# Widening an accumulating DMA to all tap pairs in a dynamic convolution followed by a tanh-shrink feed-forward layer

## Chip, cores, metric

One core of one Trainium2 chip. The metric is the device time of one execution in microseconds. The kernel before takes 768.71 us (median of 3 runs, 767.7 to 769.29).

## The reference, cut to what matters

```python
w = softmax(weight_gen, axis=-1)             # (8, 4096, 8 heads, 7 taps)
x_unf = windows of 7 past positions of x     # x: (8, 4096, 192), zeros ahead of each sequence
x = einsum('bshk,bskhg->bshg', w, x_unf).reshape(32768, 192)
h = x @ w_in                                 # (192, 2048)
out = (h - tanh(h)) @ w_out                  # (2048, 192)
```

## The kernel before

Tokens come in 32 superblocks of 1024 (8 per partition). For each, ScalarE takes the exponential of the tap weights, VectorE finishes the softmax, and GpSimd multiplies x by the weights, one product tile per tap. Seven product tiles must be summed and transposed. TensorE does both with matmuls against the identity that accumulate in PSUM ("transposes" below, line label `pc`). From superblock 4 on, an accumulating DMA first adds most of the odd taps' products into the even ones', so that TensorE has fewer to sum.

```python
ACC = NPAIR * J * D - J * R                      # all pairs but one third of the last one
...
            if k == K - 2 and in_pairs:          # in products(n), on GpSimd, after the last odd tap
                nc.gpsimd.dma_start(
                    out=even[:].rearrange("p i c j h g -> p (i c j h g)")[:, 0:ACC],
                    in_=odd[:].rearrange("p i c j h g -> p (i c j h g)")[:, 0:ACC],
                    accum_op=mybir.AluOpType.add, max_dma_last_dim=4096)
...
            groups = [even[:, i] for i in range(NPAIR)] + [last[:]]
            prods_of[n] = [groups + ([odd[:, NPAIR - 1]] if c == NC - 1 else []) for c in range(NC)]
```

Each f tile of the first matmul (16 a superblock) goes to one of three PSUM buffers, is read by tanh (ScalarE) and a subtraction (VectorE), which frees the buffer. The transposed sums use the same three buffers: chunk 2 (the "last third") between matmuls of the second layer, then chunks 0 and 1 (the "two thirds") in a burst. The softmax also parks its reciprocals in the first of these buffers.

```python
    for n in range(NTOT):
        if n + 3 < NTOT:
            load_x(n + 3)
        for p in range(J):
            gemm1(n, 2 * p); gemm1(n, 2 * p + 1)           # f tiles 2p, 2p+1
            ...
            if n + 3 < NTOT:
                if p == 1: softmax_exp(n + 3)
                if p == 1 and n + 4 < NTOT: load_wg(n + 4)
                if 2 <= p <= 5: softmax_sum(n + 3, (p - 2) * 2, (p - 1) * 2)
                if p == 6: softmax_recip(n + 3, 0, J // 2)
            if p < 6 or n == NTOT - 1: gemm2((n - 1) * J + p)
            if p == 0 and 1 < n < NTOT - 2: products(n + 2, behind=last_sub[0])
            ...
        gemm2((n - 1) * J + 6, between=between)            # last-third transposes of n + 1 in between
        conv(n + 1, (0, 1))                                # two-thirds transposes: 64 in a burst
        gemm2((n - 1) * J + 7, 0, FILL)
        if n + 3 < NTOT:
            softmax_recip(n + 3, J // 2, J)
            softmax_norm(n + 3, pcs[0][:, 0])              # copy to PSUM, then scale
        gemm1(n, NFT - 2); ...; gemm1(n, NFT - 1); ...
```

The softmax here doesn't subtract the row's maximum and nothing guards it: scores larger than these inputs give would overflow.

## Time and profile before

| | before |
|---|---|
| time, median | 768.71 us |
| span of the profiled execution | 765.5 us |
| steady superblock (start of its first tanh to the next one's) | 22.775 us |
| superblocks 1 / 2 / 3, the ramp | 28.30 / 23.91 / 22.97 us |
| accumulating DMA, issue to landing | 8.8 us |

Superblock times are read from the trace as the start of a superblock's first tanh to the start of the next one's. In the steady part nearly all agree within 0.01 us, so a change of 0.1 us per superblock is plain in the trace.

### The profile page before, as it was taken

The numbers are of one execution on the slowest core, as the hardware profiler recorded it, in microseconds if no ns is written. First come the engines' busy times: TensorE is split into PE (matmuls) and PEld (weight loads), VectorE is DVE, ScalarE is ACT, GpSimd is POOL, SyncE is SP. The second block draws the span as 40 slices with busy tenths as digits, with TensorE's granted clock in tenths as the row PEclk, the third lists the DMA queues.
The fourth block names the chain that finished last, engine by engine and source line by source line (L and its number), as shares of the span: only waits on it lengthen the run. The fifth ranks groups of instructions, "written<-read, shape, count | busy, mean of one in ns | idle before, by whom it ended". The sixth has DMA issues, their size and how long they took to land.

```text
span 765.5 us, 32560 instructions
## 1 busy us (share of the span) xinstructions
PE 739.1 (97%) x14848; PEld 564.6 (74%) x14848; DVE 681.1 (89%) x765; ACT 642.0 (84%) x869; POOL 668.9 (87%) x262
## 2 busy tenths in 40 slices
PE   4798999999999999999999999999999999999997
PEld 2476777777777777777777777777777777777777
DVE  7986899999999999999999999998999999998893
ACT  4886788888888888888888888888888888888882
POOL 8999999999999999999999999999999999999000
PEclk9999999999999999999999999999999999999999
DMA  8911467665555775545775555766555676542312
GB/s 217 236 42 57 134 171 183 182 175 121 124 151 163 182 181 117 130 150 156 182 184 129 131 144 147 182 179 151 133 131 149 173 182 169 118 122 64 81 43 85
DMA packets 25399, 110.04 MB, mean 144 GB/s; under 512 B 4671, under 2 KB 9519, under 8 KB 21294
## 3 DMA queue, kind: packets, MB, share of 16 engines
q1 hardware_dynamic: 14718, 77.03, 29.1%
q0 software_dynamic: 10544, 30.94, 25.5%
q8 instruction: 116, 1.90, 1.0%
q14 instruction: 21, 0.17, 0.1%
HBM read 54.52 MB, written 25.17 MB: 104 GB/s over the span
## 4 chain that ended last, share of the span: by engine, by line
PE 79%; DVE 15%; ACT 3%; issue 1%; DMA 1%; DVEq 0%
PE ph L308 39%; PE obank L342 37%; DVE gt L320 9%; ACT th L319 3%; DVE wsm L193 2%; PE pc L267 2%; DVE zr L163 2%; PE po L377 1%; DMA x_t<-in_x_dram 1%; DVE pc L169 1%; DVE odd L219 0%; DMA wg_t<-in_weight_gen_dram 0%; DVE even L219 0%; DVE zsum L154 0%; DVE obank L193 0%
## 5 line engine op out<-in xcount | busy, mean ns | idle before, releaser
L320 DVE TENSOR_TENSOR gt<-ph,th 128x1024 bf16<-128x1024 f32 x512 | 604.9, 1220 | 62.0 <-ACT th L319 52.8
L319 ACT ACTIVATE th<-ph 128x1024 f32<-128x1024 f32 x512 | 500.3, 1021 | 66.7 <-PE ph L308 64.8
L342 PE MATMUL obank<-w_out,gt 64*128 64x192 bf16 x7936 | 399.9, 243 | 0.8 <-ACT out_sb L361 0.4
L308 PE MATMUL ph<-convT,w_in 64*128 64x512 bf16 x3072 | 384.4, 378 | 7.9 <-DVE gt L320 2.9
L342 PEld LDWEIGHTS <-gt 64*128 64x128 bf16 x7936 | 343.6, 94 | 65.5 <-issue 0.9
L219 POOL TENSOR_TENSOR even<-x_t,wsm 128x1536 bf16<-128x1536 f32 x93 | 272.6, 2931 | 27.5 <-DVE gt L320 27.2
L219 POOL TENSOR_TENSOR odd<-x_t,wsm 128x1536 bf16<-128x1536 f32 x93 | 272.6, 2931 | 0.0
L308 PEld LDWEIGHTS <-w_in 64*128 64x128 bf16 x3072 | 163.6, 94 | 115.6 <-issue 11.7
L219 POOL TENSOR_TENSOR last<-x_t,wsm 128x1536 bf16<-128x1536 f32 x32 | 105.9, 3308 | 0.0
L361 ACT ACTIVATE out_sb<-obank 128x192 f32<-128x192 f32 x248 | 81.6, 329 | 7.0 <-PE obank L342 2.6
L291 ACT ACTIVATE convT<-pc 128x512 bf16<-128x512 f32 (+1 forms) x63 | 50.7, 807 | 30.1 <-PE pc L267 30.1
L267 PE MATMUL pc<-ident,even 64*128 64x64 bf16 x2256 | 56.1, 191 | 0.6 <-issue 0.4
L267 PEld LDWEIGHTS <-even 64*128 64x128 bf16 x2304 | 53.2, 96 | 1.4 <-issue 0.7
L234 POOL DMA_DIRECT2D even<-odd x28 | 33.7, 1205 | 8.7 <-POOL odd L219 8.7
L267 PE MATMUL pc<-ident,last 64*128 64x64 bf16 x752 | 26.8, 192 | 9.4 <-POOL last L219 9.2
L154 DVE TENSOR_REDUCE zsum<-e_t 128x16 f32<-128x112 f32 (+1 forms) x116 | 31.5, 271 | 3.0 <-ACT e_t L143 3.0
L267 PEld LDWEIGHTS <-last 64*128 64x128 bf16 x768 | 19.7, 96 | 9.7 <-POOL last L219 9.2
L143 ACT ACTIVATE e_t<-wg_t 128x448 f32<-128x448 f32 x32 | 18.5, 578 | 6.5 <-DMA wg_t<-in_weight_gen_dram 6.5
L267 PE MATMUL pc<-ident,odd 64*128 64x64 bf16 x464 | 18.5, 198 | 3.7 <-issue 2.6
L193 DVE TENSOR_TENSOR wsm<-e_t,pc 128x448 f32<-128x448 f32 x28 | 17.4, 622 | 3.1 <-DVE pc L169 0.2
L267 PEld LDWEIGHTS <-odd 64*128 64x128 bf16 x512 | 15.1, 100 | 4.6 <-issue 2.7
L163 DVE RECIPROCAL zr<-zsum 128x32 f32<-128x32 f32 (+1 forms) x58 | 16.6, 327 | 0.1
(27 smaller groups left out, 64.5 us busy)
## 6 DMA issues: line engine op xcount, KB each, us to landing
x_t<-in_x_dram SPq DMA_DIRECT2D x31, 1344.0 KB, 9.0
even<-odd POOLq DMA_DIRECT2D x28, 1024.0 KB, 8.8
out_dram<-out_sb SPq DMA_DIRECT2D x31, 768.0 KB, 11.6
wg_t<-in_weight_gen_dram SPq DMA_DIRECT2D x32, 224.0 KB, 7.8
x_t<-in_x_dram SPq DMA_DIRECT2D x1, 768.0 KB
w_out<-in_moe_w_out_dram POOLq DMA_DIRECT2D x1, 768.0 KB, 8.8
out_dram<-out_sb SPq DMA_DIRECT2D x4, 192.0 KB, 1.8
x_t<-in_x_dram SPq DMA_DIRECT2D x1, 504.0 KB
```

What stands on the lines that cost most here:

```text
L154: nc.vector.reduce_sum(out=zsum_of[n][:, j0 * H : j1 * H], in_=e_of[n][:, j0:j1].rearrange("p j h k -> p (j h) k"), axis=AX.X,)
L163: nc.vector.reciprocal(zr_of[n][:, j0 * H : j1 * H], zsum_of[n][:, j0 * H : j1 * H])
L193: return eng.tensor_mul(wsm.rearrange("p j h k -> p (j h) k"), e_t[:].rearrange("p j h k -> p (j h) k"), zr.rearrange("p (n o) -> p n o", ...
L219: mul = eng.tensor_mul(dst[k][:, :, j0:j1].rearrange("p c j h g -> p j h c g"), x_t[:, k + j0 : k + j1, :].rearrange("p j (h c g) -> p j h ...
L234: nc.gpsimd.dma_start(out=even[:].rearrange("p i c j h g -> p (i c j h g)")[:, 0:ACC], in_=odd[:].rearrange("p i c j h g -> p (i c j h g)" ...
L267: nc.tensor.matmul(pc[r][:, col : col + R] if home else pc[:, r, col : col + R], lhsT=prods[c][gi][r * R : (r + 1) * R, c, 2 * j : 2 * j + ...
L291: nc.scalar.activation(out=out, in_=pc[:, :, 0:cols].rearrange("p r (cj t) -> p r cj t", t=R), func=ACT.Copy,)
L308: nc.tensor.matmul(ph[:, r, :], lhsT=w_in[r * R : (r + 1) * R, c, f * P : (f + 1) * P], rhs=convT[r * R : (r + 1) * R, c, :], start=(c == ...
L319: last_act[0] = nc.scalar.activation(out=th[:], in_=ph_f, func=ACT.Tanh)
L320: last_sub[0] = nc.vector.tensor_sub(gt[:], ph_f, th[:])
L342: mm = nc.tensor.matmul(po[:, 0:D], lhsT=g_of[n][f][r * R : (r + 1) * R, col : col + P], rhs=w_out[r * R : (r + 1) * R, f, :], start=(r == ...
L361: last_act[0] = nc.scalar.activation(out=out_sb[:, j, :], in_=po[:, 0:D], func=ACT.Copy)
```

## The change

Intent: the DMA adds all three odd tiles into the even ones, as three pieces of 1536 elements a partition instead of two of 2048, so that the last third needs 32 transposes and not 40. With it come two changes of order: the softmax pieces, and the load of the tap weights (cut from the diff below), move one or more p earlier, and the x loads made in superblocks 1 to 3 go to the end of the superblock, behind the convolution.

```diff
-    ACC = NPAIR * J * D - J * R
...
-                    out=even[:].rearrange("p i c j h g -> p (i c j h g)")[:, 0:ACC],
-                    in_=odd[:].rearrange("p i c j h g -> p (i c j h g)")[:, 0:ACC],
+                    out=even[:].rearrange("p i c j h g -> p i (c j h g)"),
+                    in_=odd[:].rearrange("p i c j h g -> p i (c j h g)"),
...
-            prods_of[n] = [
-                groups + ([odd[:, NPAIR - 1]] if c == NC - 1 else []) for c in range(NC)
-            ]
+            prods_of[n] = [[even[:, i] for i in range(NPAIR)] + [last[:]]] * NC
...
+    LATE = (1, 2, 3)
...
-        if n + 3 < NTOT:
+        if n + 3 < NTOT and n not in LATE:
             load_x(n + 3)
...
-                if p == 1:
+                if p == 0:
                     softmax_exp(n + 3)
...
-                if 2 <= p <= 5:
-                    softmax_sum(n + 3, (p - 2) * 2, (p - 1) * 2)
-                if p == 6:
-                    softmax_recip(n + 3, 0, J // 2)
+                if 1 <= p <= 3:
+                    softmax_sum(n + 3, (p - 1) * 3, min(p * 3, J))
+                if 4 <= p <= 5:
+                    softmax_recip(n + 3, (p - 4) * JH, (p - 3) * JH)
...
-            softmax_recip(n + 3, J // 2, J)
...
+        if n in LATE:
+            load_x(n + 3, last_conv[0])
```

More of the change, by code (lines that the diff above doesn't have):

```diff
@@ L81 @@
     last_exp = {}
+    last_conv = {}
     first_halo = {}
@@ L242, in products @@
         if in_pairs:
-            groups = [even[:, i] for i in range(NPAIR)] + [last[:]]
-            prods_of[n] = [
-                groups + ([odd[:, NPAIR - 1]] if c == NC - 1 else []) for c in range(NC)
-            ]
+            prods_of[n] = [[even[:, i] for i in range(NPAIR)] + [last[:]]] * NC
         else:
@@ L290, in conv_out @@
             else:
-                nc.scalar.activation(
+                last_conv[0] = nc.scalar.activation(
                     out=out,
@@ L498 @@
             if n + 3 < NTOT:
-                if p == 1:
+                if p == 0:
                     softmax_exp(n + 3)
-                if p == 1 and n + 4 < NTOT:
+                if p == 0 and n + 4 < NTOT:
                     load_wg(n + 4)
-                if 2 <= p <= 5:
-                    softmax_sum(n + 3, (p - 2) * 2, (p - 1) * 2)
-                if p == 6:
-                    softmax_recip(n + 3, 0, J // 2)
+                if 1 <= p <= 3:
+                    softmax_sum(n + 3, (p - 1) * 3, min(p * 3, J))
+                if 4 <= p <= 5:
+                    softmax_recip(n + 3, (p - 4) * JH, (p - 3) * JH)
             if p < 6 or n == NTOT - 1:
```

## The prediction

> **What bounds the kernel now.** I read the page first, then the chain of waits inside one steady superblock, then the ScalarE timeline of that superblock against one near the end, then the ramp.
>
> ```profile
> PE 739.1 (97%) x14848; PEld 564.6 (74%) x14848; DVE 681.1 (89%) x765; ACT 642.0 (84%) x869; POOL 668.9 (87%) x262
> ...
> PE 79%; DVE 15%; ACT 3%; issue 1%; DMA 1%; DVEq 0%
> ```
>
> TensorE is busy nearly always, but a fifth of the chain that ends last is not TensorE. So not every matmul removed is time removed. The next view is the chain of waits between 309.9 and 321 us (columns: start, us, what), the end of superblock 12; superblocks repeat every 22.775 us there (the first tanh of each to the next).
>
> ```profile
> 311.23 0.67 PE ph L308 x6
> ...
> 311.91 1.03 ACT th L319
> ...
> 312.97 2.35 DVE gt L320 x2
> 315.33 0.48 DVE zr L163 x2
> ...
> 315.90 0.24 DVE pc L169
> ...
> 316.23 0.63 DVE wsm L193
> ...
> 316.91 0.82 PE ph L308 x6
> ```
>
> The transposes (L267) run in this stretch and are **not on the chain**: it leaves TensorE after f tile 12 of the first matmul, goes through tanh, two subtractions, two reciprocals, the copy and the softmax scaling, and returns with f tile 15. That tile needs the PSUM buffer in which the softmax keeps its reciprocals, and TensorE waits 0.36 us for it (24 such waits, 8.5 us in the waits view). Next the ScalarE timeline of superblock 12 (start, us, ...):
>
> ```profile
> 311.91 1.94 ACT L319 ACTIVATE th<-ph 128x1024 f32<-128x1024 f32 x2 [0.32 <-PE ph L308]
> ...
> 315.40 1.02 ACT L291 ACTIVATE convT<-pc 128x1024 bf16<-128x1024 f32 x1 [0.36 <-PE pc L267]
> 316.32 1.02 ACT L319 ACTIVATE th<-ph 128x1024 f32<-128x1024 f32 x1
> 317.77 1.02 ACT L319 ACTIVATE th<-ph 128x1024 f32<-128x1024 f32 x1 [0.44 <-PE ph L308]
> ...
> 321.61 1.02 ACT L319 ACTIVATE th<-ph 128x1024 f32<-128x1024 f32 x1 [0.32 <-PE ph L308]
> ```
>
> and of superblock 30, which has no softmax to do for a later one:
>
> ```profile
> 721.88 1.94 ACT L319 ACTIVATE th<-ph 128x1024 f32<-128x1024 f32 x2 [0.32 <-PE ph L308]
> ...
> 725.36 1.02 ACT L291 ACTIVATE convT<-pc 128x1024 bf16<-128x1024 f32 x1 [0.36 <-PE pc L267]
> 726.28 2.17 ACT L319 ACTIVATE th<-ph 128x1024 f32<-128x1024 f32 x2
> ...
> 731.44 1.02 ACT L319 ACTIVATE th<-ph 128x1024 f32<-128x1024 f32 x1 [0.32 <-PE ph L308]
> ```
>
> From tanh of tile 12 to tanh of the next superblock's tile 2 is 9.70 us with the softmax and 9.56 without. The trace thus already holds a superblock without the 0.36 us wait, and it is only **0.14 us** shorter. Last, the chain in superblock 1, and under it the busy times of 61.6 to 65 us (clock is the 0.54):
>
> ```profile
> 57.83 1.21 PE pc L267 x83
> 59.04 2.61 issue
> 61.65 0.95 PE pc L267 x29
> ...
> 61.60:65.00 3.40, 3.35 (x55) 2.58 (x56) 0.00 (x0) 1.78 (x2) 3.40 (x2) 0.54 0.27 72
> ```
>
> Superblock 1 takes 28.30 us. TensorE stops 2.61 us among transposes whose operands were ready (GpSimd had finished them at 54.2) and then runs at half clock.
>
> **What the Trainium skill says.** (1) "Runtime: NRT & Kernel Launch", Instruction fetch mechanics: instructions arrive in 16 KiB blocks over the sequencer's own DMA queue, mostly hidden. The page agrees on the size (116 instruction packets, 1.90 MB); at 59.04 it is, as I read it, not hidden. (2) "DMA: Bandwidth & Descriptors", Issuing engines are not separate DMA queues: all transfers share the same 16 engines. The x load is issued at 54.27, lands at 59.83, and from 55.5 to 59 the DMA share is 0.83; an instruction packet runs only at 59.37. (3) "TensorE: Matmul & The Clock Gate", Part 1: an idle window of about 3.4 us halves the clock. The trace has one such halving between ramp and end, 3.41 us long, right after this pause. (4) The DMA page again, SDMA does more than copy: the adder takes at most 2048 elements a piece. The build agrees: the accumulate is 128x2x2048 before, 128x3x1536 after.
>
> **The change part by part.**
>
> Transposes. 64 of them run from 314.26 to 315.19, so 14.5 ns each (two row tiles at once; the 191 ns of the groups view is latency). Eight fewer is 0.116 us of TensorE in the last-third sums, 28 x 0.116 = 3.2 us if it all counted. It lands just before the two-thirds sums, which need the PSUM buffer of tile 12. VectorE frees that at 314.20 and TensorE starts at 314.26: it is already tied. Start earlier and it waits. Worth about 0.01 us a superblock.
>
> Reciprocals. In the new order the three sums (3, 3 and 2 rows) and two reciprocals go to the pairs p=1 to 5. After tile 13's subtraction (ends 315.33) only copy and scaling are left. They end at about 316.20 instead of 316.85, so tile 15 starts when TensorE gets there: tile 14 at 315.38 + 0.645 + 7 pairs x 0.0826 = 316.60, not 316.91; 0.31 us gained. Two tiles later it meets the next wait: the next superblock's tile 1 needs tile 14's buffer, whose chain (transposes done, 1.02 ScalarE copy, 1.02 tanh, 1.22 subtraction, ending 318.60) is untouched. TensorE could be there at 318.48 but starts at 318.65, against 318.79 before. So 0.14 us stays: the same number that superblock 30 shows.
>
> Do the moved VectorE pieces fit? A pair period is 2.615 us. The sum of two rows took 0.26 and left 0.084 idle. Three rows are 168 elements; between 0.26 for 112 and 0.61 for 448 that is 0.32, so about 0.02 is left. A reciprocal of 0.26 to 0.34 just fits. The exponential (0.58) at p=0 falls in a ScalarE hole of the new order. No charge.
>
> Steady sum: 28 x 0.14 = 3.9 us.
>
> Accumulate. 1.18 MB for 1.05 and 24 pieces an engine for 16. Landing was 8.8 us; scaled by bytes and piece counts I estimate 9.5 to 10. It is issued at 317.22 and needed near 335.5: hidden. Its 1.2 us on GpSimd hardly depends on the pieces (the w_out load with 2048 rows took 1.23), and GpSimd idles 1.13 us a superblock waiting for its pace.
>
> Late x loads (superblocks 1, 2, 3). The loads go behind the convolution, so the DMA engines are free while superblock 1's transposes drink instructions fastest. Without trouble that superblock should take 22.775 + 64 extra transposes x 14.5 ns = 23.7 us: 4.6 us are in play, 2.61 of pause, 1.7 of half clock (half of 3.41), the rest small. GpSimd reaches these tiles at 75.3, 96.5 and 118.0; the loads should land near 70, 88 and 114 by adding 9 us to the new issue points, so nothing waits. I count three quarters: 3.5 us.
>
> Sum: 768.7 - 3.9 - 3.5 = **761.3 us**.
>
> **Rivals.** *All transposes count*: 3.2 us from the transposes and 8.5 from the wait, plus the ramp, 753 us. Against it: superblock 30 shows the wait removed and 0.14 gained. *The pause is not fetch contention*: then only the steady part comes, 765 us. For it: the profile says only "issue". Against it: later transposes at the same rate do not pause (no issue wait over 0.3 us from 100 to 650 us). *GpSimd or the accumulate becomes the bound*: GpSimd's work repeats every 21.6 us in the ramp; if descriptor generation doubled to 2.4, it would be 22.8 and eat the gain, 766 to 769. A small form is likely: with superblock 1 shorter, superblock 3 wants the first accumulate at about 103, and it landed at 101.56 already before growing; a wait under 1 us, once. *VectorE slips* because a 3-row sum overruns its hole: up to 0.05 us a pair, recovered at p=0: 1 us.
>
> **Range and chances.** Steady part 3 to 5, ramp 0 to 4.6, less up to 1.5 for the last two rivals: 758 to 766 in 8 of 10. A 2% gain needs below 753.6, all of the first rival: 0.03. Slower than 2% needs a new stall each superblock: 0.01.
>
> **What would show it.** Right: steady period 22.63 us; the wait of tile 15 on the scaling gone; new short waits of TensorE on subtractions at tile 1 and ahead of the two-thirds sums; no 2.6 us issue pause and no half clock near 60 us. Wrong: a period near 22.3 (transposes count), a pause that survives or moves, transposes waiting for the accumulate, or GpSimd without its 1.1 us pace idle.

## The result

The changed kernel takes 765.28 us (median of 4 runs, 764.66 to 766.12) against 768.27 us for the kernel before on the same chip; ratio 0.996, 95% interval 0.9943 to 0.9978. The gain is 3.0 us where 7.4 were forecast.

The page of the changed kernel, the lines that answer to the first two of the prediction:

```profile
PE 739.3 (97%) x14624; PEld 572.9 (75%) x14624; DVE 676.4 (89%) x737; ACT 642.2 (84%) x869; POOL 671.0 (88%) x262
...
PE 82%; POOL 13%; DMA 2%; issue 2%; ACT 0%; SPq 0%; DVE 0%; POOLq 0%
```

There are 224 matmuls fewer, VectorE has left the chain, and GpSimd (POOL) has come onto it. TensorE's busy time has not fallen at all. The ScalarE timeline of a steady superblock (start, us, what, and in brackets the idle time before and who ended it):

```profile
290.23 1.94 ACT L316 ACTIVATE th<-ph 128x1024 f32<-128x1024 f32 x2 [0.32 <-PE ph L305]
...
293.71 1.02 ACT L288 ACTIVATE convT<-pc 128x1024 bf16<-128x1024 f32 x1 [0.47 <-PE pc L264]
294.63 2.18 ACT L316 ACTIVATE th<-ph 128x1024 f32<-128x1024 f32 x2
...
299.79 1.94 ACT L316 ACTIVATE th<-ph 128x1024 f32<-128x1024 f32 x2 [0.16 <-PE ph L305]
```

Tanh of tile 12 to tanh of the next superblock's tile 2 is 299.79 - 290.23 = 9.56 us, the forecast value, and the period is 22.63 us from superblock 8 on. So the steady half of the forecast came exactly. The rest is in the ramp. Superblock times in us, from the two traces:

```
superblock            1      2      3      4      5      6      7   8 and on
before            28.30  23.91  22.97  22.77  22.77  22.78  22.77  22.775 (two at 22.92)
changed           25.29  24.09  22.67  24.02  22.67  26.36  22.46  22.63
difference        -3.02  +0.19  -0.31  +1.25  -0.11  +3.58  -0.31  about -0.14 each
```

Superblocks 7 to 28 gain 3.58 us together; 29 and 30 lose 0.16. The start and superblocks 1 to 6, taken together, **lose** 1.8 us, against a forecast gain of 3.5: what superblock 1 gave, superblocks 4 and 6 took back. (The two profiled executions differ by 1.6 us and not by 3.0; the kernel before's was the quickest of its first four, 767.27 us. Only the profiled ones can be taken apart.) The chain of waits of the changed kernel at the end of superblock 6 (start, us, what), and the busy times of the 3.4 us after it (0.50 is the granted clock, 0.02 the DMA share):

```profile
175.91 0.47 PE pc L264 x25
176.39 1.92 issue
178.30 0.74 PE pc L264 x39
...
179.00:182.40 3.40, 3.40 (x34) 2.08 (x28) 0.76 (x1) 2.05 (x2) 3.40 (x2) 0.50 0.02 5
```

This is the picture that superblock 1 of the kernel before showed: TensorE stops amid its burst of transposes for nothing the profile knows of, then runs 3.41 us at half clock. It has moved, not gone. Superblock 4 has two smaller losses. First the waits of GpSimd from 92 to 112 us, then the chain from 126 to 136 us:

```profile
POOL odd L219 <- DMA even<-odd: 3.8, 1, 3.8
```

```profile
118.56 9.66 DMA even<-odd
128.21 0.14 issue
...
129.82 0.38 PE pc L264 x26
130.20 0.77 issue
130.96 0.73 PE pc L264 x38
```

GpSimd, about to write the odd products of superblock 5 at 100.1 us, waits 3.8 us until the accumulating DMA of superblock 4 lands, a wait that the kernel before has not. So it issues the next DMA at 118.6 us and not 114.4, and that one lands at 128.2, after TensorE has come for its sums. The DMA also lands later than before, counted over all of them (issue lines of the changed kernel: KB each, median us from issue to landing; 8.8 us before):

```profile
even<-odd POOLq DMA_DIRECT2D x28, 1152.0 KB, 10.4
```

### The profile page after: what moved, and what is told of

Its sections match the earlier page's. It is cut to its first block, busy times and chain, and to the rows that moved or that the text cites. A ratio compares the mean times of both kernels' runs of the same rounds, so it can differ in the third digit from the quotient of the medians.

```text
span 763.9 us, 32085 instructions
## 1 busy us (share of the span) xinstructions
PE 739.3 (97%) x14624; PEld 572.9 (75%) x14624; DVE 676.4 (89%) x737; ACT 642.2 (84%) x869; POOL 671.0 (88%) x262
## 4 chain that ended last, share of the span: by engine, by line
PE 82%; POOL 13%; DMA 2%; issue 2%; ACT 0%; SPq 0%; DVE 0%; POOLq 0%
PE obank L340 38%; PE ph L305 38%; PE pc L264 5%; POOL odd L219 5%; POOL even L219 5%; POOL last L219 2%; PE po L375 1%; DMA even<-odd 1%; DMA x_t<-in_x_dram 1%; POOL wsm L193 0%; POOL w_in L415 0%; POOL w_out L402 0%; SPq L96 0%; DVE out_sb L387 0%; ACT ot L386 0%
## 5 line engine op out<-in xcount | busy, mean ns | idle before, releaser
L305 PE MATMUL ph<-convT,w_in 64*128 64x512 bf16 x3072 | 392.5, 379 | 4.7 <-DVE gt L317 2.5
L340 PEld LDWEIGHTS <-gt 64*128 64x128 bf16 x7936 | 351.5, 94 | 59.0 <-ACT th L316 0.9
L305 PEld LDWEIGHTS <-w_in 64*128 64x128 bf16 x3072 | 172.9, 94 | 107.7 <-issue 19.6
L264 PE MATMUL pc<-ident,even 64*128 64x64 bf16 x2256 | 59.4, 191 | 3.7 <-issue 3.0
L264 PEld LDWEIGHTS <-even 64*128 64x128 bf16 x2304 | 56.6, 96 | 7.8 <-issue 4.2
L234 POOL DMA_DIRECT2D even<-odd x28 | 36.1, 1289 | 8.6 <-POOL odd L219 8.6
L154 DVE TENSOR_REDUCE zsum<-e_t 128x24 f32<-128x168 f32 (+2 forms) x88 | 27.5, 312 | 2.8 <-ACT e_t L143 2.8
L163 DVE RECIPROCAL zr<-zsum 128x32 f32<-128x32 f32 (+1 forms) x58 | 20.3, 350 | 0.1
L375 PE MATMUL po<-w_out,gt 64*128 64x192 bf16 x256 | 11.0, 243 | 0.0
L375 PEld LDWEIGHTS <-gt 64*128 64x128 bf16 x256 | 10.8, 93 | 0.0
## 6 DMA issues: line engine op xcount, KB each, us to landing
even<-odd POOLq DMA_DIRECT2D x28, 1152.0 KB, 10.4
```

The costliest lines, as they stand in the source:

```text
L154: nc.vector.reduce_sum(out=zsum_of[n][:, j0 * H : j1 * H], in_=e_of[n][:, j0:j1].rearrange("p j h k -> p (j h) k"), axis=AX.X,)
L163: nc.vector.reciprocal(zr_of[n][:, j0 * H : j1 * H], zsum_of[n][:, j0 * H : j1 * H])
L234: nc.gpsimd.dma_start(out=even[:].rearrange("p i c j h g -> p i (c j h g)"), in_=odd[:].rearrange("p i c j h g -> p i (c j h g)"), accum_o ...
L264: nc.tensor.matmul(pc[r][:, col : col + R] if home else pc[:, r, col : col + R], lhsT=prods[c][gi][r * R : (r + 1) * R, c, 2 * j : 2 * j + ...
L305: nc.tensor.matmul(ph[:, r, :], lhsT=w_in[r * R : (r + 1) * R, c, f * P : (f + 1) * P], rhs=convT[r * R : (r + 1) * R, c, :], start=(c == ...
L340: mm = nc.tensor.matmul(po[:, 0:D], lhsT=g_of[n][f][r * R : (r + 1) * R, col : col + P], rhs=w_out[r * R : (r + 1) * R, f, :], start=(r == ...
```

## The experiments

**Theory A**, formed on these lines: the missing gain went into the one 3.8 us wait of GpSimd, which put the later DMAs into the transposes of superblocks 4 and 6. Why the wait is new: the kernel before also read `odd` with TensorE, much later than the DMA does; now the DMA alone reads it. In the built program the odd products of superblock 5 wait for that DMA, where before they waited for TensorE. As I read it, the two-buffer pool hands superblock 5 the buffer whose reading ended first in program order, now that of superblock 4. **Rivals**: B, the wider DMA starves TensorE's instruction fetch by itself; C, the transposes do count; D, the pauses have nothing to do with loads.

**1. Two odd buffers by parity** (changed kernel otherwise).

```diff
-        odd = ppool.tile([P, NPAIR, NC, J, H, GC], BF16, name="odd")
+        odd = ppool.tile([P, NPAIR, NC, J, H, GC], BF16, name="odd", tag=f"odd{n % 2}", bufs=1)
```

> The changed kernel, with the odd products in two buffers chosen by the superblock's parity, so that superblock 5 takes the buffer of superblock 3 and not that of superblock 4, which the accumulating DMA is still reading. Theory A (the missing gain went into one 3.8 us wait of GpSimd for that DMA, which put the later DMAs into the transposes of superblocks 4 and 6): the 3.8 us wait is gone, superblocks 4 and 6 take 22.6 to 22.9 us each and not 24.0 and 26.4, and the time falls from 765.3 to about 760.3. Rival B (the 12% more bytes and the smaller pieces of the DMA delay the instruction fetch by themselves): the wait goes but pauses remain, 764 to 766.

Measured: 763.69 us, ratio to before 0.9927 (0.9906 to 0.9947). GpSimd's wait is gone (no such line from 64 to 111 us) and superblock 6 takes 22.47 us. But superblock 4 takes 24.55 and superblock 5 24.02, with pauses of TensorE of 1.96 and 1.55 us from one matmul's start to the next. The buffer is the cause of the wait; theory A as a whole is too simple, since the pauses only moved and the expected 760.3 us did not come.

**2. The softmax order alone** (kernel before, with the p conditions of the diff above).

> The kernel before, with only the softmax pieces moved (exponential at p=0, sums at p=1 to 3, reciprocals at p=4 and 5); all 24 last-third transposes per tap stay. Theory A: the whole steady gain is from this, superblock period 22.63 to 22.64 us and not 22.775, about 764.4 us (3.9 less than before). Rival C (the transposes carry part of the gain): period between 22.65 and 22.775.

Measured: 765.62 us, ratio 0.9952 (0.9933 to 0.9971). Steady period 22.64 us with all its transposes: 0.14 us less than before, and 0.004 more than the changed kernel. The steady gain is all from the softmax order. Superblock 1 fell by 2.05 us and superblock 2 rose by 3.51, with a new pause and half clock at 87.3 us, although no load was moved.

**3. The wide accumulate alone** (kernel before, with the DMA and `prods_of` lines of the diff).

> The kernel before, with only the accumulate widened to all the pairs and its 8 transposes dropped. Theory A: the steady period stays 22.775 us, GpSimd waits once for the DMA of superblock 4 before it writes the odd products of superblock 5, and the time is not below before: 767.5 to 773. Rival C: the 8 transposes of 14.5 ns count, period 22.66, 765.

Measured: 770.96 us, ratio 1.002 (1.000 to 1.004). Steady period 22.775 us, as before: **eight transposes fewer are worth nothing**. GpSimd's wait is there, from its waits between 84 and 112 us:

```profile
POOL odd L219 <- DMA even<-odd: 4.0, 1, 4.0
```

Superblocks 4 and 5 take 24.16 and 24.31 us. The part that names the change gains nothing by itself; what it costs, 1.0 us between the medians with an interval that touches no change, is in the ramp.

**4. The late x loads alone** (kernel before, with LATE).

> The kernel before, with only the x loads of superblocks 1 to 3 put behind the convolution. Theory A: the 2.6 us pause and the half clock of superblock 1 go, that superblock takes about 25.3 us and not 28.3, steady period 22.775, 765.3 us. Rival D (the pause has nothing to do with the load): superblock 1 keeps 28 us, 768.3.

Measured: 765.21 us, ratio 0.9947 (0.9924 to 0.9969). Superblock 1 takes 24.73 us; its chain of waits:

```profile
59.30 1.21 PE pc L268 x83
60.51 0.49 issue
61.00 0.59 PE pc L268 x29
```

The pause at the same transpose is 0.49 us and not 2.61, so rival D falls: the load made most of it (superblock 1 also began 1.5 us later here; theory E below has the same border in ten traces). Superblocks 2, 4 and 5 give back 0.5 us each, with small pauses.

**Theory A2**, after these: TensorE's pauses come when its bursts meet DMA traffic whose times GpSimd sets; an earlier TensorE meets it elsewhere.

**5. Softmax order and late loads, narrow accumulate** (2 and 4 together).

> The changed kernel without its widened accumulate (softmax pieces moved and x loads of superblocks 1 to 3 put late; the 8 transposes stay). Theory A2 (the gain of the early superblocks is given back where TensorE's transposes meet DMA traffic whose times GpSimd sets; the wide accumulate adds to that traffic): superblocks 4 and 5 take about 23.2 us each as with the late loads alone, steady 22.64, about 762.5 us, so faster than the changed kernel although it has 224 more transposes. Rival (the 12% wider accumulate does not matter, TensorE is simply early): 24 us or more in superblocks 4 and 5, 764 us or more.

Measured: 762.92 us, ratio 0.9936 (0.9906 to 0.9965); one of its four runs took 766.81 us and the others 762.83 to 763.00, so a single execution can stand 4 us apart. Superblocks 4 and 5 take 23.12 and 23.19 us, as expected. The changed kernel's ratio of 0.996 came from another call, so I don't rank the two by it; superblocks 4 to 6 sum to 68.9 us here and 73.1 us there.

**6. Late loads in superblocks 4 and 5 too, on 1, and 7. on 5** (`LATE = (1, 2, 3, 4, 5)`).

> The changed kernel with the parity buffers and with the x loads of superblocks 4 and 5 late as well. Theory A2: without an x load in flight the pauses of superblocks 4 and 5 (1.96 and 1.55 us with the parity buffers alone) shrink below 0.5 us, both superblocks take 22.6 to 23.1 us, total about 761. Rival (the accumulate or the store alone starves the fetch): the pauses stay, 763.5.

> The narrow accumulate with the softmax pieces moved and the x loads of superblocks 1 to 5 late. Theory A2: no pause over 0.5 us after superblock 2, superblocks 4 and 5 at 22.6 to 22.9 us, about 760.5 us, the fastest of all here; the steady period is 22.64 as with the wide accumulate. Rival: pauses elsewhere, 762 or more.

Measured: 766.99 us, ratio 0.9978 (0.9958 to 0.9997), and 765.39 us, ratio 0.9954 (0.993 to 0.9979). In both, superblocks 4 and 5 take 22.63 or 22.64 us, no pause left: that step holds. But GpSimd now starts superblock 8 late, 6.9 us in the wide one and 5.0 us in the narrow one. In the wide one x itself landed at 160.6 us, before GpSimd was free at 161.9; the small DMA of zeros that follows it at the start of a sequence landed at 168.7, and there the wait ended. GpSimd's next DMAs move (186.3 us for the fifth in the wide one, 180.5 in experiment 1), and pauses come in superblocks 6 to 9 (23.48, 26.41, 23.50, 24.51 us in the wide one). The total I expected was wrong by 5 to 6 us.

**8. x loads put into the bursts on purpose** (experiment 1, and for n of 8 and on `load_x(n + 3, last_act[0])` at p = 4).

> The changed kernel with parity buffers and with the x loads of superblocks 8 on put on purpose at p=4, so that each is in flight while the transposes run. Theory A2: pauses by issue of 0.5 to 2.5 us appear in the transposes of most superblocks that showed none, the period rises from 22.63 to between 23 and 26 us, the time to 775 to 840 us. Rival D (the pauses are not made by loads): period stays 22.63, 764 us.

Measured in one look, so its state is unknown: 765.39 us. The median period stays 22.63 us, with two pauses over 0.5 us after the ramp (1.04 us at 269 us and 0.55 us at 566 us), though the load is issued at 308.9 in a superblock whose burst is near 313. So a load in flight is not enough, and theory A2 falls in this form: something else must coincide.

**Theory E.** The trace also records the packets by which instructions come. Over all 17 traces I took every gap of over 0.5 us between the starts of two matmuls, from 55 to 740 us, that the profile puts down to issue. There are 48. A few, with the end of the last instruction packet before it:

```
kernel            TensorE resumes   last instruction packet ended   difference
before                  61.65                60.33                    1.33 us
changed                 60.32                59.07                    1.25
changed                130.96               129.69                    1.27
changed                178.30               176.97                    1.33
parity buffers         131.50               130.06                    1.44
all 48                                                        1.21 to 1.60, median 1.40
```

A pause ends a fixed time after a packet, so it is a wait for instructions. Counting the instructions shows the same: if those of TensorE (weight loads, matmuls, semaphore instructions) are numbered in each trace, all 48 pauses resume at the same place of a block of 256, 38 at remainder 194 and 10 at 193. That place is called the border below. A burst of 64 transposes is 128 instructions in 0.93 us, half a 16 KiB packet (256 instructions by the block size that the Trainium skill's "Runtime: NRT & Kernel Launch" gives under Instruction fetch mechanics; 116 packets for 29,696 weight loads and matmuls before agree). A late packet hurts when its border falls just ahead of or in a burst.

How late a packet comes can be read too, as the time from TensorE's passing the border before it to the packet's start. Over the 17 traces (1785 borders, from superblock 1 on) the median is 3.60 us while an accumulating DMA is in flight (596 borders) and 0.75 us otherwise. It is 3.58 us with the narrow accumulate and 3.60 with the wide one. At the border where the kernel before pauses in superblock 1 it is 1.9 to 2.8 us in the three traces that load x there, and 0.4 to 1.0 us in the seven that load it late with the border unmoved. These counts were made after all the runs, and no run takes the accumulate away.

If a pause needs a border in the wrong place, the same work with the borders shifted must pause elsewhere.

**9 to 12. Borders shifted.** Idle transposes of the identity ahead of the first real ones, where TensorE has nothing to do; two instructions each. 9: 32 on the changed kernel. 10: 64 on the changed kernel. 11: 12 on the parity buffers. 12: 64 on the parity buffers.

```diff
+        if n == 0:
+            for _ in range(32):
+                nc.tensor.matmul(pcs[0][:, 0, 0:R], lhsT=ident[0:R, :], rhs=ident[0:R, 0:R], start=True, stop=True)
```

> The changed kernel with 32 idle transposes of the identity (64 instructions) ahead of everything on TensorE, where it has nothing to do, so that every later 16 KiB block of its instructions begins 64 instructions earlier in the work; loads, GpSimd and DMAs are as they were. Theory E (a pause is an instruction block that comes late into the transposes, so it depends on where the block's border falls): the pauses of superblocks 4 and 6 (0.96 and 2.10 us) change by over 0.5 us or move to other superblocks, steady period 22.63, time anywhere from 761 to 767. Rival A2 (only the DMA traffic's times decide): pauses of superblocks 4 and 6 stay within 0.3 us, time 765.

> The same with 64 idle transposes (128 instructions, half a block). A steady superblock has about 3.5 blocks, so theory E expects the roles of even and odd superblocks to change places: the pause leaves superblock 6 (22.6 us there) and may come in 5 or 7; rival A2 keeps it at 26.4 us.

> The changed kernel with parity buffers, and 12 idle transposes (24 instructions) ahead, which puts the block borders of superblock 4 about where the narrow accumulate with late loads has them (it has 16 more instructions per superblock). If the narrow one's smaller pauses (0.52 and 0.61 us against 1.96 and 1.55) come from the borders, superblocks 4 and 5 take about 23.2 us here; if they come from the narrower DMA, they stay near 24.5 and 24.0.

> The parity buffers with 64 idle transposes. Theory E: superblocks 4 and 5 change by over 0.5 us from 24.55 and 24.02. Rival A2: they stay within 0.3 us.

Measured, with the superblock times of the traces:

```
                          time    ratio  (interval)           1      2      4      5      6      7
changed, no shift        765.28   0.996  (0.9943-0.9978)  25.29  24.09  24.02  22.67  26.36  22.46
 9 changed, 64           764.92   0.996  (0.9931-0.9989)  24.46  23.57  22.63  23.23  22.63  23.92
10 changed, 128          763.64   0.9944 (0.9915-0.9973)  24.45  23.57  27.14  22.47  22.63  22.63
 1 parity, no shift      763.69   0.9927 (0.9906-0.9947)  25.18  24.14  24.55  24.02  22.47  22.63
11 parity, 24            763.29   0.9939 (0.9902-0.9976)  25.16  24.66  23.08  23.20  22.47  22.63
12 parity, 128           761.71   0.9919 (0.989-0.9947)   24.46  23.57  24.69  22.47  22.63  22.63
```

Theory E passes on its main point: no load, no DMA and no GpSimd instruction was moved in the program, and the pauses of superblocks 1, 2, 4, 5, 6 and 7 came and went.

But only 10 and 12 isolate the border: their superblock 1 starts within 0.15 us of the unshifted kernel's, and the pauses of superblocks 1 and 2, and of 6 in the one and 5 in the other, are gone. In 9 and 11 superblock 0 took 22.7 and 22.8 us, not 20.6, and TensorE came to superblock 1 3.8 and 2.3 us later. Experiment 8 shows what that can do without any shift. Up to superblock 8 its program is that of experiment 1 and no border is moved, but superblock 0 happened to take 22.8 us, and superblocks 4 and 5 took 22.97 and 22.66 us where experiment 1 has 24.55 and 24.02.

Experiment 10 is as expected in superblock 6, but superblock 7 has no pause in exchange. Experiment 11 came as expected: with borders where the narrow accumulate has them, the wide one gives 23.08 and 23.20 us, as the narrow one did (23.12 and 23.19). But TensorE came late in that run, which could have done as much (experiment 8), so it doesn't show that the borders did it. Rival B falls all the same, in its strong form: beside the wide accumulate the pauses of superblocks 4 and 5 stayed under 0.5 us in experiment 8, and packets are no later beside it than beside the narrow one (3.60 and 3.58 us). Experiment 12 missed in part: superblock 5 changed by 1.55 us, but superblock 4 by only 0.14, its pause being 2.26 us instead of 1.96. Experiment 10 shows the loss that the width and the buffer do make once the pauses are out of the way; its chain in superblock 4:

```profile
116.95 12.01 DMA even<-odd
128.96 0.14 issue
129.10 0.24 PE pc L273 x4
```

TensorE waits 2.5 us for this DMA and falls to half clock from 129.5 us: 27.14 us for the superblock. With the parity buffers (12) the wait is not there.

**13 to 15. Parity buffers, borders shifted by 64, 96 and 192 instructions** (32, 48 and 96 idle transposes), to see if the whole expected gain comes out when neither stands in the way.

> Parity buffers and 32 idle transposes (64 instructions) ahead. Theory E with the GpSimd lag gone: superblocks 1 to 4 as in the 64-instruction shift of the changed kernel (24.5, 23.6, 22.7, 22.6), at most one pause after that, 759 to 761.5 us, below the 761.7 of the 128 shift. If a pause needs only DMA traffic, superblocks 4 and 5 are near 24 again and it is 763.5.

> The same with 48 idle transposes (96 instructions). Theory E: the borders lie between the 64 and the 128 shift; 759 to 763 us, steady period 22.63, and every pause over 0.5 us without a DMA wait ends 1.2 to 1.6 us after an instruction packet.

> The same with 96 idle transposes (192 instructions). Theory E: a different set of pauses again, 759 to 766 us, steady period 22.63.

Measured: 761.68 us, ratio **0.9912** (0.9897 to 0.9927); 762.24 us, 0.9918 (0.9903 to 0.9934); 763.92 us, 0.9944 (0.9927 to 0.996). The 64 shift missed its range, 759 to 761.5 us, by 0.2; the other two are in theirs. With 64 and 96, superblocks 1 to 6 take 24.45, 23.87, 22.67, 22.83, 22.67, 22.63 and 24.45, 23.57, 22.67, 22.86, 22.67, 22.63 us. The waits of the 64 shift from 54 to 190 us, those by issue (total, times, longest):

```profile
PEld L316 <- issue: 1.8, 6, 0.3
...
PEld L351 <- issue: 0.3, 1, 0.3
PEld L275 <- issue: 0.2, 1, 0.2
PE obank L351 <- issue: 0.2, 1, 0.2
```

No wait of the matmuls themselves (PE) by issue is over 0.2 us. With 192, pauses of 1.40, 1.10 and 1.65 us are back in superblocks 1, 2 and 4. The 64 shift gains 6.8 us by its ratio (0.0088 x 768.5), and the forecast for the change was 7.4. In its trace, 1.6 us are lost before superblock 1; superblock 0 took 22.2 us there against 20.5, with two stretches of half clock before 27 us. With the 96 and the 128 shift (0.9918, 0.9919) it has the lowest ratio here. All three are faster than the kernel before. The intervals of 64 and 96 lie below the changed kernel's (0.9943 to 0.9978), that of 128 overlaps it slightly, and they come from other calls, so that ranking is weaker.

## Why the prediction was wrong

**Right: what bounds a steady superblock.** The forecast period was 22.63 us; it is 22.63. The wait of tile 15 is gone, and the next one caps the gain, as superblock 30 of the kernel before had shown. In the changed kernel tile 1 of the next superblock starts 0.37 us after the matmul ahead of it, in nearly every steady superblock. The softmax order alone does all this (experiment 2).

**Right: the eight transposes.** "About 0.01 us a superblock": 0.00 with the accumulate alone (experiment 3). The two-thirds sums wait for tile 12's buffer instead: in the changed kernel they start 0.18 us after the matmul ahead, and 0.08 before.

**Wrong: the term "Late x loads".** The step that failed is "the loads should land near 70, 88 and 114 ..., so nothing waits. I count three quarters: 3.5 us". In superblock 1 the sum was nearly right, 3.0 us, and the one late load whose landing the trace has, that of superblock 3, landed at 114.7 us. But the forecast treated the pause as an event of that one superblock, with a load to blame. The traces and experiments 8 to 15 show a pause to be a late instruction packet whose border meets a burst; a change of instruction count or timing, or just another execution, can deal these meetings anew. The changed kernel drew 0.8 us in superblock 4 and 1.9 us plus a half clock in superblock 6. These two packets started 3.9 and 4.5 us after the border before, with an accumulating DMA still in flight; in the kernel before, the DMA had landed 3.8 and 4.8 us ahead of TensorE at the same borders, and there was no pause. Start and superblocks 1 to 6 together came out at +1.8 us, not -3.5. The time, 765.28 us, still lies in the range of 758 to 766, but by luck: the ramp came out worse than the range allowed for it. The prediction's own sign of being wrong, "a pause that survives or moves", is what came. In the 64 shift with the parity buffers, superblock 1 gives 3.85 us and superblocks 2 to 6 take none back, though 1.6 us were lost before superblock 1: the gain was there, and in the changed kernel it was given back later.

**Wrong in a smaller way: the accumulate.** The landing time was estimated at 9.5 to 10 us; it is 10.4. GpSimd's cost was forecast unchanged from 1.2 us and is 1.29. A wait of "under 1 us, once" was named for the first one, and 0.4 us came, at the second. What the forecast did not see is that with TensorE no longer reading `odd`, the buffers would be handed out in another order. That made the 3.8 us wait of GpSimd, and it can cost TensorE 2.5 us and a half clock (experiment 10). VectorE did not slip.

**Open.** That the x load delayed superblock 1's packet is shown by experiment (2.61 against 0.49 us of pause). That an accumulate in flight delays packets by some 3 us is read from the traces and was not put to a test; how it does so is not shown. Why superblock 0 takes 22 to 23 us in some executions is open too. Experiment 8, which shifts nothing, has it as well, with half clock from 24.5 to 28.0 us, so it does not need a shift.

## What to carry to other kernels

Before counting a removed instruction as time, look for a place in the same trace where the thing is already missing; here the last superblocks held the answer to 0.01 us. When a buffer loses one of its readers, check in the built program which earlier user its next writer now waits for. In a long unrolled program with bursts of short instructions, a difference of a few microseconds may be the draw of the instruction blocks: shift them with a few idle instructions, look at more than one execution, and compare again, before crediting or blaming the edit.

## What the Trainium skill lacked or had wrong

- "Runtime: NRT & Kernel Launch", Instruction fetch mechanics, calls the cost of crossing a 16 KiB boundary mostly hidden. In these runs 48 gaps between matmul starts, of 0.5 to 2.8 us, ended 1.21 to 1.60 us after an instruction packet, all at one place of a 256-instruction block; shifting the blocks by 128 instructions took superblock 6 from 26.36 to 22.63 us. Beside an accumulating DMA a packet started 3.60 us after the border before, otherwise 0.75 us (medians).
- "TensorE: Matmul & The Clock Gate", Part 1, ties the half clock to an idle window of about 3.4 us. A pause of 1.92 us was followed by 3.41 us at half clock (changed kernel, superblock 6), while one of 2.40 us (experiment 6) was not.
- "DMA: Bandwidth & Descriptors", SDMA does more than copy, names the adder but no rate. The accumulate took 8.8 us from issue to landing for 1024 KB in pieces of 2048 elements, and 10.4 us for 1152 KB in pieces of 1536, beside other traffic.
